# A Fourier layer split as 49 by 64 in place of 56 by 56, with two buffers for a low part, a shared buffer and a merged addition

## The chip, the cores and the metric

The kernel runs on one core of one Trainium2 chip. The metric is the device time of one execution in microseconds. Before the change it is 1770.43 us, the median of three runs (1767.99 to 1770.92).

## What is computed

```python
X = np.fft.rfft(x, axis=1)                # x: (8, 3136, 256) float32
Yr = Xr @ w_r - Xi @ w_i + b_r
Yi = Xr @ w_i + Xi @ w_r + b_i
Yr = np.sign(Yr) * np.maximum(np.abs(Yr) - lam, 0.0)   # lam = 0.01; Yi alike
y = np.fft.irfft(Yr + 1j * Yi, n=3136, axis=1)
h = np.maximum(y @ w_in, 0.0)             # 256 -> 1024
gate = sigmoid(conv(h))                   # three taps along the sequence
out = (h * gate) @ w_out                  # 1024 -> 256
```

The real transform runs over 3136 points of each of 8 batches and 256 columns. The spectrum is mixed by a complex 256 by 256 matrix, thresholded and transformed back. A gated feed-forward block with a convolution of three taps follows.

## The kernel before, in words

**The transform by matrices.** 3136 = 56 x 56. A transform of 3136 points is done as two short ones: `stage1` (L239) transforms over one index of 56 points, with two columns j of the other index at once (112 rows), and writes 28 frequencies u to the DRAM array sc1. `stage2` (L273) transforms over the other index for one u at a time, by plain float32 matmuls whose stationary operand is the data and whose moving operand is the table t2 (128 columns). `mix` (L291) multiplies by the complex matrix in three products (c = 2, 0, 1), in float32r with a high and a low part of each operand (fh and fl, wmix_hi and wmix_lo), 36 matmuls of 256 columns; it adds the biases, thresholds and splits the result v into sh and sl. `stage3` (L324) is the first half of the way back, 12 matmuls, and writes to the DRAM array sc2. `stage4` (L416) reads sc2 across the u, does the second half and leaves the sequence of one batch in SBUF as yh and yl.

**Work items.** A group of stage 1 takes JC = 4 columns j, so a batch has 28/4 = 7 groups, each with two matmuls of 512 columns (L245) into one PSUM buffer, two copies on ACT (L246), and one store from a1 to sc1 (L247). An item (b, g) of stages 2, mix and 3 takes UG = 4 of the 28 u: 7 items per batch, 56 in all. Its input a2 is loaded from sc1 by L270; since an item needs all j of its batch, the first load of a batch waits for the last store of stage 1 of that batch. Stage 4 has 7 groups per batch, each with a load of z2 (L419) through three buffers, 8 matmuls (L423), a copy on ACT (L429) and a subtraction on DVE (L430).

**Thresholding (L305 to L321).** p1 holds the common product ps[2] plus the bias, one addition for the real and one for the imaginary part (L309); four additions over 64 rows form v (L313). ACT computes r = relu(v - lam) (L318), DVE ends with v = min(v + lam, r) (L319), ACT casts it to sh (L320) and POOL subtracts to sl (L321). p1, r and sl have one buffer each, v and sh two.

**Order.** The loop (L373) runs over the items with stage 2 of item `it`, mix of `it - 1` and stage 3 of `it - 3`; new stage-1 groups are asked for ahead of the items that need them (L386). A scheduler then fixes the order of each engine from these priorities; each engine works its list strictly in order. All loads and stores go through SP's list, where a DMA waits for its data or buffer and holds back those behind it. The weights are split in the background (`later`, L207). A head (`stage1_head`, L249) does batch 0's groups at once with all of its tiles in SBUF.

**The feed-forward part** runs in steps of `up` (L432, 12 matmuls of 450 columns) and `down` (L463, 21 matmuls of 256), 224 steps, with a stage-4 group of the next batch in three of eight steps until the batch is done. At its start stand the groups of batch 0 and two of batch 1.

Of the kernel before, what the change touches and what calls it, by code (L numbers as in the profile page):

```python
# [9 lines left out]
F32 = mybir.dt.float32  # L10
F32R = mybir.dt.float32r
# [7 lines left out]
B, S, D, FF = 8, 3136, 256, 1024  # L19
R = 56  # L20
U = 28
SL = 57
SP = 64
H = 28
LAM = 0.01
UG = 4
NG = U // UG
JC = 4
P = 128
# [5 lines left out]
def _tables():  # L35
    n = np.arange(R)
    u = np.arange(U)

    f = np.zeros((R, 2, U))
# [3 lines left out]
    f[:, 1, 0] = np.where(n % 2 == 0, 1.0, -1.0)  # L43
    fwd1 = np.zeros((2, R, U, 2, 2))
    for h in range(2):
        fwd1[h, :, :, :, h] = f.transpose(0, 2, 1)

    g = np.transpose(f, (1, 2, 0)).copy()
    g[:, 1:, :] *= 2.0
    g /= S  # L50
    inv2 = np.zeros((2, 2 * U, R, 2))
    for i in range(2):
        inv2[i, :, :, i] = g.reshape(2 * U, R)
    fwd2 = np.zeros((2, R, U, 2, SP))
    inv1 = np.zeros((2, SP, U, 2, R))
    for uu in range(U):
        for s in range(SL):
            if uu == 0:
                c = 0 if s < 29 else 1
                k = R * s if s < 29 else 28 + R * (s - 29)  # L60
                th = 2 * np.pi * ((k * n) % S) / S
                sn, cs = np.sin(th), np.cos(th)
                edge = k in (0, S // 2)
                if edge:
                    sn = np.zeros(R)
                    cs = np.round(cs)
                w = 1.0 if edge else 2.0
                fwd2[c, :, 0, 0, s] = cs
                fwd2[c, :, 0, 1, s] = -sn
                inv1[0, s, 0, c, :] = w * cs  # L70
                inv1[1, s, 0, c, :] = -w * sn
            elif s < R:
                k = uu + R * s
                th = 2 * np.pi * ((k * n) % S) / S
                sn, cs = np.sin(th), np.cos(th)
                sg = 1.0 if k <= S // 2 else -1.0
                fwd2[0, :, uu, 0, s] = cs
                fwd2[1, :, uu, 0, s] = sn
                fwd2[0, :, uu, 1, s] = -sn * sg
                fwd2[1, :, uu, 1, s] = cs * sg  # L80
                inv1[0, s, uu, 0, :] = cs
# [6 lines left out]
    return {
        "fwd1": fwd1.transpose(1, 0, 2, 3, 4).reshape(2 * R, 2 * R).astype(np.float32),
        "fwd2": fwd2.reshape(2 * R, U * 2 * SP).astype(np.float32),  # L90
        "inv1": inv1.reshape(2 * SP, U, 2, 2, H).transpose(0, 1, 4, 3, 2).reshape(2 * SP, U * 2 * R).astype(np.float32),
        "inv2": inv2.reshape(2 * R, 2 * R).astype(np.float32),
    }
# [3 lines left out]
def spectral_ffn_kernel(ctx: ExitStack, tc: tile.TileContext, x, w_r, w_i, b_r, b_i,  # L97
                        w_in, conv_w, w_out, fwd1, fwd2, inv1, inv2, out):
    nc = tc.nc
    K1, K2 = 2 * R, 2 * SP  # L100
# [3 lines left out]
    sc2 = [dram.tile([K1, U, D], F32, name=f"sc2_{b}") for b in range(B)]  # L104

    cst = ctx.enter_context(tc.tile_pool(name="cst", bufs=1))


    i2 = cst.tile([K1, K1], F32, name="i2")
    cw = cst.tile([P, 3, NF], F32, name="cw")  # L110
# [6 lines left out]
    with ExitStack() as ab:  # L117
# [12 lines left out]
        f1 = c1.tile([K1, P], F32, name="f1")[:, 0:K1]  # L130
        t2 = c1.tile([K1, U, K2], F32, name="t2")
# [136 lines left out]
        def load_a2(b, g):  # L268
            a2 = a2p.tile([K1, UG, D], F32, name="a2")
            ld = nc.sync.dma_start(a2, sc1[b].rearrange("(u q) j d -> (q j) u d", q=4)[:, g * UG:(g + 1) * UG, :])  # L270
            return a2, ld

        def stage2(g, a2):  # L273

            fh, fl = [wkf.tile([P, NT, 3, UG, SP], F32R, name=nm) for nm in ("fh", "fl")]
            d = wkf.tile([P, NT, UG, SP], F32, name="d", bufs=DB)
            for t in range(NT):
                ps = ps2.tile([P, UG, 2, SP], F32, name="ps_s2")
                for k in range(UG):
                    nc.tensor.matmul(ps[:, k], a2[:, k, t * P:(t + 1) * P], t2[:, g * UG + k, :],  # L280
                                     start=(k == 0), stop=(k == UG - 1), skip_group_check=True)
# [6 lines left out]
            nc.vector.tensor_tensor(fl[:, :, 2], d, fh[:, :, 2].bitcast(F32), op=ALU.subtract)  # L288
            return fh, fl

        def mix(xs):  # L291
# [15 lines left out]
            half = (slice(0, SP), slice(SP, K2))  # L307
            for c in range(2):
                nc.vector.tensor_tensor(p1[:, c], ps[2], bias[:, c], op=ALU.add)  # L309
            for c in range(2):  # L310
# [13 lines left out]
        def stage3(b, g, s):  # L324

            sh, sl, _ = s
            ps = psa.tile([K1, UG, D], F32, name="ps_s3")
            for k in range(UG):
                u = g * UG + k
                for n, (lt, rh) in enumerate(((i1_hi, sh), (i1_hi, sl), (i1_lo, sh))):  # L330
                    nc.tensor.matmul(ps[:, k, :], lt[:, u, :], rh[:, k, :], start=(n == 0), stop=(n == 2))  # L331
# [73 lines left out]
    JG = 4  # L405
# [135 lines left out]
```

## Time and profile before

| what | value |
|---|---|
| median of three runs | 1770.43 us (1767.99 to 1770.92) |
| the profiled execution | 1769.05 us, span 1767.3 us |
| mean granted clock of TensorE | 0.995 |
| busy share: PE, weight load, DVE, ACT, POOL | 98%, 92%, 86%, 70%, 8% |
| stage 1, head and after | 14 and 98 matmuls, the last one near 475 us |
| spectral part | to about 549 us |
| first `up` | 574 us |
| DMA, whole span | 164.63 MB, mean 93 GB/s |

PE is TensorE's matmul queue, PEld its weight loads, DVE VectorE, ACT ScalarE, POOL GpSimd, SP the engine whose queue issues the DMAs. In a group of instructions `a<-b` means that tile a is written from tile b; L280 is line 280. "Idle before" names what released an engine after it had stood still. A plain float32 matmul shows as two records. The chain that ended last follows, from the end backwards, at each step what the work had waited for.

### The profile page before, as it was taken

How to read it: one execution, taken by the hardware profiler on the slowest of the kernel's cores; microseconds unless marked ns; L12 is line 12 of the kernel's file. 1: busy time of each engine (PE TensorE's matmuls, PEld its weight loads, DVE VectorE, ACT ScalarE, POOL GpSimd, SP SyncE). 2: the span in 40 equal slices, each digit the busy share in tenths (PEclk: the TensorE clock that was granted, in tenths of full speed). 3: DMA queues.
4: the chain of work that ended last, by engine and by line, in shares of the span. 5: the costliest groups of instructions: out<-in, count | busy, mean ns of one | idle time of the engine just before them, and what ended most of it. 6: DMA issues, size and time to landing. Idle time of an engine off the chain costs nothing.

```text
span 1767.3 us, 29387 instructions
## 1 busy us (share of the span) xinstructions
PE 1731.0 (98%) x12096; PEld 1621.6 (92%) x12096; DVE 1524.3 (86%) x1820; ACT 1229.1 (70%) x1590; POOL 134.7 (8%) x60
## 2 busy tenths in 40 slices
PE   6899999999998999999999999999999999999999
PEld 2788888888998999999999999999999999999998
DVE  2899999998896988988888888888888888888887
ACT  2667777776665777777777777777777777777766
POOL 0122222222232000000000000000000000000000
PEclk8999999999999999999999999999999999999999
DMA  9777677677534110111111011111101111100001
GB/s 263 216 230 236 196 232 216 192 230 228 164 111 136 43 43 22 32 53 53 32 53 53 22 55 51 49 46 52 43 22 43 53 43 43 42 22 22 22 22 42
DMA packets 107382, 164.63 MB, mean 93 GB/s; under 512 B 8816, under 2 KB 86000, under 8 KB 107248
## 3 DMA queue, kind: packets, MB, share of 16 engines
q1 hardware_dynamic: 107248, 162.74, 30.9%
q8 instruction: 96, 1.57, 0.4%
q14 instruction: 38, 0.31, 0.1%
HBM read 85.65 MB, written 77.07 MB: 92 GB/s over the span
## 4 chain that ended last, share of the span: by engine, by line
PE 93%; DMA 3%; DVE 1%; ACT 1%; issue 0%; SPq 0%; ACTq 0%
PE acc L470 31%; PE ps_h L442 31%; PE ps_mx L304 12%; PE ps_s L423 5%; PE ps_s L280 5%; PE ps_s L331 4%; PE ps_s L245 4%; DMA i_raw<-in_inv_dram 2%; DMA z<-sc 1%; DMA sc<-ha 0%; DMA a<-sc 0%; DMA sc<-a 0%; ACT a L246 0%; DVE cw L212 0%; DVE yl L430 0%
## 5 line engine op out<-in xcount | busy, mean ns | idle before, releaser
L470 PE MATMUL acc<-wout,gh 128*128 128x256 f32 x3136 | 567.0, 280 | 0.0
L451 DVE SCALAR_TENSOR_TENSOR c<-h,cw,c 128x896 f32<-128x896 f32 x448 | 513.1, 1147 | 47.3 <-ACT c L449 46.3
L442 PE MATMUL ps_h<-yh,win 128*128 128x450 f32 x1792 | 551.0, 368 | 0.1
L470 PEld LDWEIGHTS acc<-wout,gh 128*128 128x128 f32 x3136 | 493.7, 188 | 6.5
L470 PE MATMUL acc<-wout,gl 128*128 128x256 f32 x1568 | 437.6, 281 | 0.0
L444 ACT ACTIVATE h<-ps_h 128x900 f32<-128x900 f32 x224 | 207.7, 927 | 254.8 <-PE ps_h L442 254.8
L442 PEld LDWEIGHTS ps_h<-yh,win 128*128 128x128 f32 x1792 | 338.7, 189 | 26.4 <-DVE yl L430 0.8
L442 PE MATMUL ps_h<-yl,win 128*128 128x450 f32 x896 | 329.2, 367 | 0.0
L470 PEld LDWEIGHTS acc<-wout,gl 128*128 128x128 f32 x1568 | 293.7, 188 | 0.1
L457 DVE TENSOR_TENSOR gl<-c,gh 128x896 fp32r<-128x896 f32 x224 | 243.1, 1089 | 53.6 <-ACT gh L456 50.1
L453 DVE TENSOR_TENSOR c<-h,c 128x896 f32<-128x896 f32 x224 | 243.6, 1088 | 46.9 <-ACT c L452 46.7
L456 ACT CAST gh<-c 128x896 fp32r<-128x896 f32 x224 | 209.8, 942 | 49.4 <-DVE c L453 49.4
L452 ACT ACTIVATE c<-c 128x896 f32<-128x896 f32 x224 | 213.3, 952 | 23.9 <-DVE c L451 21.0
L304 PE MATMUL ps_mx<-wmix_lo,fh 128*128 128x256 f32 x672 | 202.2, 301 | 0.0
L304 PE MATMUL ps_mx<-wmix_hi,fh 128*128 128x256 f32 x672 | 196.9, 294 | 0.5 <-DVE v L313 0.3
L304 PE MATMUL ps_mx<-wmix_hi,fl 128*128 128x256 f32 x672 | 188.7, 282 | 1.3 <-DVE fl L288 1.2
L442 PEld LDWEIGHTS ps_h<-yl,win 128*128 128x128 f32 x896 | 168.9, 189 | 11.0
L449 ACT ACTIVATE c<-h,cw 128x896 f32<-128x896 f32 x168 | 175.5, 1044 | 2.6 <-DVE gl L457 0.2
L321 POOL TENSOR_TENSOR sl<-v,sh 128x1024 fp32r<-128x1024 f32 x56 | 134.5, 2402 | 423.1 <-PE ps_s L331 300.0
L313 DVE TENSOR_TENSOR v<-ps_mx,p 64x512 f32<-64x512 f32 x224 | 154.0, 688 | 3.3
L304 PEld LDWEIGHTS ps_mx<-wmix_lo,fh 128*128 128x128 f32 x672 | 126.4, 188 | 12.3 <-issue 12.3
L304 PEld LDWEIGHTS ps_mx<-wmix_hi,fl 128*128 128x128 f32 x672 | 126.0, 188 | 11.8 <-issue 9.9
(84 smaller groups left out, 2023.0 us busy)
## 6 DMA issues: line engine op xcount, KB each, us to landing
a<-sc SPq DMA_DIRECT2D x56, 448.0 KB, 5.0
sc<-z SPq DMA_DIRECT2D x56, 448.0 KB, 3.3
z<-sc SPq DMA_DIRECT2D x56, 448.0 KB, 3.8
xr<-in_x_dram SPq DMA_DIRECT2D x55, 448.0 KB, 4.7
out_dram<-o SPq DMA_DIRECT2D x27, 896.0 KB, 4.0
sc<-a SPq DMA_DIRECT2D x49, 448.0 KB, 4.9
sc<-ha SPq DMA_DIRECT2D x7, 448.0 KB, 7.5
win_bits<-in_moe_w_in_dram SPq DMA_DIRECT2D x4, 512.0 KB, 7.6
```

The source lines that it names most:

```text
L304: nc.tensor.matmul(ps[c][:, k, :], lt, rh, start=(n == 0), stop=(n == len(mm) - 1))
L313: nc.vector.tensor_tensor(v[dst, :, k, :], ps[c][src], p1[src, c], op=ALU.add)
L321: SL_ENG.tensor_tensor(sl, v, sh.bitcast(F32), op=ALU.subtract)
L442: nc.tensor.matmul(ps[:, a, 0:CH + 2], lt, rh, start=(n == 0), stop=(n == len(mm) - 1))
L444: nc.scalar.activation(h, ps[:, :, 0:CH + 2], AF.Relu)
L449: nc.scalar.mul(c, h[:, :, 0:CH], cw[:, 0, f:f + 1])
L451: nc.vector.scalar_tensor_tensor(c, h[:, :, k:k + CH], cw[:, k, f:f + 1], c, op0=ALU.mult, op1=ALU.add)
L452: nc.scalar.activation(c, c, AF.Sigmoid)
L453: nc.vector.tensor_tensor(c, h[:, :, 1:CH + 1], c, op=ALU.mult)
L456: nc.scalar.copy(gh, c)
L457: nc.vector.tensor_tensor(gl, c, gh.bitcast(F32), op=ALU.subtract)
L470: nc.tensor.matmul(acc[m // 2][:, m % 2, :], lt[:, sl], rh[:, f, :], start=(f == 0 and n == 0 and m % 2 == 0), stop=(f == NF - 1 and n == ...
```

## The change

The sequence is split as 49 x 64. Stage 1 now transforms over 49 points (R) with 98 rows and 32 pairs of columns j (H), which makes 8 groups of 4 per batch, 64 in all. There are 25 frequencies u, 0 to 24. Since 49 is odd, none but u = 0 is special: u = 1 to 24 fill 6 whole items per batch, and u = 0 of four batches is gathered into one item, which makes 8 x 6 + 2 = 50 items. The second index has 64 points, so that stage 2 has 128 rows and stage 3 writes 128 rows (64 rows are read for u = 0). Stage 4 reads 100 rows (25 x 4), has a moving operand of 98 columns and 8 groups per batch. 

Besides, one addition over 1024 elements, with ps[2] read twice, takes the place of the two of L309; sl gets a second buffer; r takes the memory of p1. The rule that asks for new stage-1 groups lets two per item in at first and four per three items later, for one and a half and then one.

```diff
-R = 56
-U = 28
-SL = 57
+R = 49
+R2 = 64
+U = 24
 SP = 64
-H = 28
+H = 32
...
         def load_a2(b, g):
-            a2 = a2p.tile([K1, UG, D], F32, name="a2")
-            ld = nc.sync.dma_start(a2, sc1[b].rearrange("(u q) j d -> (q j) u d", q=4)[:, g * UG:(g + 1) * UG, :])
+            a2 = a2p.tile([KQ, UG, D], F32, name="a2")
+            if g < NG:
+                rows = slice(g * 4 * UG, (g + 1) * 4 * UG)
+                ld = nc.sync.dma_start(a2, sc1[b][rows].rearrange("(u q) j d -> (q j) u d", q=4))
+            else:
+                for k in range(UG):
+                    ld = nc.sync.dma_start(a2[0:R2, k, :], sc1[b + k][4 * U:K1].rearrange("q j d -> (q j) d"))
             return a2, ld
...
                 for k in range(UG):
-                    nc.tensor.matmul(ps[:, k], a2[:, k, t * P:(t + 1) * P], t2[:, g * UG + k, :],
+                    rows, u = (KQ, g * UG + k) if g < NG else (R2, U)
+                    nc.tensor.matmul(ps[:, k], a2[0:rows, k, t * P:(t + 1) * P], t2[0:rows, u, :],
                                      start=(k == 0), stop=(k == UG - 1), skip_group_check=True)
...
-            for c in range(2):
-                nc.vector.tensor_tensor(p1[:, c], ps[2], bias[:, c], op=ALU.add)
+            nc.vector.tensor_tensor(p1, ps[2].unsqueeze(1).broadcast_to([K2, 2, UG // 2, D]), bias, op=ALU.add)
...
-            sl = wk.tile([K2, UG, D], F32R, name="sl", bufs=1)
-            r = wk.tile([K2, UG, D], F32, name="r", bufs=1)
+            sl = wk.tile([K2, UG, D], F32R, name="sl")
+            r = p1.rearrange("p c k d -> p (c k) d")
...
-            nc.sync.dma_start(sc2[b][:, g * UG:(g + 1) * UG, :], z1)
+            if g < NG:
+                nc.sync.dma_start(sc2[b][:, g * UG:(g + 1) * UG, :], z1)
+            else:
+                for k in range(UG):
+                    nc.sync.dma_start(sc2[b + k][:, U, :], z1[:, k, :])
...
-        AHEAD = NG + 3
         items = [(b, g) for b in range(B) for g in range(NG)]
+        for b in (0, UG):
+            items.insert(items.index((b + UG - 1, 0)), (b, NG))
...
-            while p1 < n_it and p1 < min(it + AHEAD, NG + 2 + it + it // 2):
-                stage1(*items[p1])
+            while p1 < min(len(firsts), NQ + 2 + 2 * it, NQ + 5 + 4 * it // 3):
+                stage1(*firsts[p1])
                 p1 += 1
```

**What the change moves.** On PE, at the turn from batch 4 to batch 5: before, stage 3 of an item (L331), one matmul of stage 1 of the next batch (L245), then the first stage 2 of batch 5 (L280, reading the tile a_3803) and its mix (L304).

```order
L331 MATMUL ps_s_3990<-sh,i_hi 112x256
L331 MATMUL ps_s_3990<-sl,i_hi 112x256
L331 MATMUL ps_s_3990<-sh,i_lo 112x256
L245 MATMUL ps_s_4009<-xr,f_113 112x512
L280 MATMUL ps_s_4026<-t_114,a_3803 128x128 x4
L280 MATMUL ps_s_4035<-t_114,a_3803 128x128 x4
L304 MATMUL ps_mx_4048<-wmix_hi,fh 128x256
```

The same place in the new order; L342 is stage 3, L251 stage 1, L292 stage 2 (a_3438 is the first tile of batch 5).

```order
L342 MATMUL ps_s_3847<-sh,i_hi 128x256
L342 MATMUL ps_s_3847<-sl,i_hi 128x256
L342 MATMUL ps_s_3847<-sh,i_lo 128x256
L251 MATMUL ps_s_3326<-xr,f_113 98x512
L251 MATMUL ps_s_3429<-xr,f_113 98x512
L342 MATMUL ps_s_3952<-sh,i_hi 128x256
L292 MATMUL ps_s_3669<-t_114,a_3438 128x128 x4
L292 MATMUL ps_s_3678<-t_114,a_3438 128x128 x4
L251 MATMUL ps_s_3432<-xr,f_113 98x512
L342 MATMUL ps_s_3952<-sl,i_hi 128x256
```

Stage 2 of the new batch has moved up to the end of the old batch's stage 3, with no mix left in front of it. On SP at the same place, the x load, the last two stores of stage 1 of batch 5 (to sc_5), the store of z (to sc_4) and the loads of the first items of batch 5:

```order
L247 DMA sc_5_62<-a_3685 112x1024
L334 DMA sc_4_69<-z_3788 112x1024
L236 DMA xr<-in_x_dram 112x1024
L247 DMA sc_5_62<-a_3793 112x1024
L270 DMA a_3803<-sc_5_62 112x4x256
L270 DMA a_3911<-sc_5_62 112x4x256
L334 DMA sc_4_69<-z_3895 112x1024
```

And in the new order, with L253 the store of stage 1, L346 that of z and L278 the load:

```order
L242 DMA xr<-in_x_dram 98x1024
L253 DMA sc_5_62<-a_3312 98x1024
L346 DMA sc_4_69<-z_3754 128x1024
L278 DMA a_3438<-sc_5_62 128x4x256
L278 DMA a_3544<-sc_5_62 128x4x256
L242 DMA xr<-in_x_dram 98x1024
L278 DMA a_3664<-sc_5_62 128x4x256
```

The load still stands close behind the last store; what moved is how much PE has queued between the two. On DVE, late in the spectral part, before (L309 the two bias additions, L319 the end of the item before them, L288 a subtraction of stage 2):

```order
L309 TENSOR_TENSOR p_5733<-ps_mx_5696,bias 128x512 x2
L319 SCALAR_TENSOR_TENSOR v<-v,r 128x1024
L288 TENSOR_TENSOR fl<-d,fh 128x2x256
L313 TENSOR_TENSOR v<-ps_mx_5694,p_5733 64x2x256 x2
L313 TENSOR_TENSOR v<-ps_mx_5695,p_5733 64x2x256 x2
```

The same in the new order (L330 ends an item, L320 is the merged addition of the next):

```order
L330 SCALAR_TENSOR_TENSOR v<-v,p_5071 128x1024
L300 TENSOR_TENSOR fl<-d,fh 128x2x256
L320 TENSOR_TENSOR p_5164<-ps_mx_5127,bias 128x1024
L324 TENSOR_TENSOR v<-ps_mx_5125,p_5164 64x2x256 x2
L324 TENSOR_TENSOR v<-ps_mx_5126,p_5164 64x2x256 x2
```

The end of an item now stands ahead of the next item's bias addition, and the two additions are one. Counted over the whole order of PE, the matmuls that stand between the start of the last stage-1 matmul of a batch and the first stage 2 that reads that batch's own item (without that first matmul itself) are:

| batch | before: mix, stage 3, stage 1, stage 2 | new: mix, stage 3, stage 1, stage 2 |
|---|---|---|
| 1 | 56, 12, 2, 0 | 0, 24, 4, 0 |
| 2 | 62, 24, 3, 8 | 36, 13, 2, 0 |
| 3 | 62, 24, 3, 8 | 19, 22, 3, 2 |
| 4 | 62, 24, 3, 8 | 41, 24, 2, 0 |
| 5 | 62, 24, 3, 8 | 0, 18, 3, 0 |
| 6 | 62, 24, 3, 8 | 34, 24, 2, 0 |
| 7 | 62, 24, 0, 8 | 34, 24, 0, 2 |

Six items stand behind the last stage 1 in the new order. At the turn to the feed-forward part ten stage-4 groups (8 of batch 0, two of batch 1) stand in front of the first `up`, for nine before.

More of the change, by code (lines that the diff above doesn't have):

```diff
@@ L42, in _tables @@
     f[:, 1, :] = -np.sin(ang)
-    f[:, 1, 0] = np.where(n % 2 == 0, 1.0, -1.0)
-    fwd1 = np.zeros((2, R, U, 2, 2))
+    fwd1 = np.zeros((R, 2, 2 * R))
     for h in range(2):
-        fwd1[h, :, :, :, h] = f.transpose(0, 2, 1)
+        for uu in range(1, U + 1):
+            for c in range(2):
+                fwd1[:, h, (uu - 1) * 4 + c * 2 + h] = f[:, c, uu]
+        fwd1[:, h, 4 * U + h] = f[:, 0, 0]
     g = np.transpose(f, (1, 2, 0)).copy()
@@ L50, in _tables @@
     g /= S
-    inv2 = np.zeros((2, 2 * U, R, 2))
+    g = np.roll(g, -1, axis=1)
+    inv2 = np.zeros((2, 2 * (U + 1), R, 2))
     for i in range(2):
[L53 to L57, printed above, removed]
+        inv2[i, :, :, i] = g.reshape(2 * (U + 1), R)
+    fwd2 = np.zeros((2, R2, U + 1, 2, SP))
+    inv1 = np.zeros((2, SP, U + 2, 2, R2))
+    for uu in range(U + 1):
+        at = (uu - 1) % (U + 1)
+        for s in range(SP):
+            k = uu + R * s
+            th = 2 * np.pi * ((k * n2) % S) / S
+            sn, cs = np.sin(th), np.cos(th)
@@ new lines, in _tables @@
+                fwd2[0, :, at, 1, s] = -sn
+                inv1[0, s, at, 0, :] = w * cs
+                inv1[1, s, at, 0, :] = -w * sn
+            else:
+                sg = 1.0 if k <= S // 2 else -1.0
+                fwd2[0, :, at, 0, s] = cs
+                fwd2[1, :, at, 0, s] = sn
+                fwd2[0, :, at, 1, s] = -sn * sg
+                fwd2[1, :, at, 1, s] = cs * sg
+                inv1[0, s, at, 0, :] = cs
+                inv1[0, s, at, 1, :] = sn
+                inv1[1, s, at, 0, :] = -sg * sn
+                inv1[1, s, at, 1, :] = sg * cs
@@ L86, in _tables @@
+    inv1[:, :, U + 1] = inv1[:, :, U]
     inv1[:, :, 1::2] = inv1[::-1, :, 1::2]
     return {
[L89 to L92, printed above, removed]
+        "fwd1": fwd1.reshape(2 * R, 2 * R).astype(np.float32),
+        "fwd2": fwd2.reshape(2 * R2, (U + 1) * 2 * SP).astype(np.float32),
+        "inv1": inv1.reshape(2 * SP, U + 2, 2, 2, H).transpose(0, 1, 4, 3, 2).reshape(2 * SP, (U + 2) * 2 * R2).astype(np.float32),
+        "inv2": inv2.reshape(4 * (U + 1), 2 * R).astype(np.float32),
@@ L99, in spectral_ffn_kernel @@
     nc = tc.nc
-    K1, K2 = 2 * R, 2 * SP
+    K1, K2, KQ, KI = 2 * R, 2 * SP, 2 * R2, 4 * (U + 1)
     dram = ctx.enter_context(tc.tile_pool(name="dram", bufs=1, space=DRAM))
     sc1 = [dram.tile([K1, H, D], F32, name=f"sc1_{b}") for b in range(B)]
-    sc2 = [dram.tile([K1, U, D], F32, name=f"sc2_{b}") for b in range(B)]
+    sc2 = [dram.tile([KQ, U + 1, D], F32, name=f"sc2_{b}") for b in range(B)]
     cst = ctx.enter_context(tc.tile_pool(name="cst", bufs=1))
-    i2 = cst.tile([K1, K1], F32, name="i2")
+    i2 = cst.tile([KI, 112], F32, name="i2")[:, 0:K1]
     cw = cst.tile([P, 3, NF], F32, name="cw")
@@ L130, in spectral_ffn_kernel @@
         f1 = c1.tile([K1, P], F32, name="f1")[:, 0:K1]
-        t2 = c1.tile([K1, U, K2], F32, name="t2")
+        t2 = c1.tile([KQ, U + 1, K2], F32, name="t2")
         cmx.tile([P, 96], F32, name="pad")
@@ L165, in load_inv1 @@
         def load_inv1(g):
-            raw = stg.tile([K2, UG, K1], F32, name="i1_raw", tag="raw", bufs=2)
-            sl = slice(g * UG, (g + 1) * UG)
+            sl = slice(g * UG, min((g + 1) * UG, U + 2))
+            raw = stg.tile([K2, sl.stop - sl.start, KQ], F32, name="i1_raw", tag="raw", bufs=2)
             nc.sync.dma_start(raw, inv1v[:, sl, :])
@@ L338, in spectral_ffn_kernel @@
         nc.scalar.activation(warm, warm, AF.Sigmoid)
-        AHEAD = NG + 3
         items = [(b, g) for b in range(B) for g in range(NG)]
+        for b in (0, UG):
+            items.insert(items.index((b + UG - 1, 0)), (b, NG))
         n_it = len(items)
+        firsts = [(b, jc) for b in range(B) for jc in range(NQ)]
         WP0, CW_IT = 3, 9
         a2s = {}
-        p1 = NG
+        p1 = NQ
         load_f1()
@@ L348, in spectral_ffn_kernel @@
             xh = []
-            for p in range(NG):
+            for p in range(NQ):
                 xr, ld = load_x(hx, 0, p, parts=2 if p == 0 else 1, tag=f"hx{p}")
@@ L368, in spectral_ffn_kernel @@
         wk.tile([P, 72], F32, name="pad", bufs=1)
-        i1_hi = cab.tile([K2, U, K1], F32R, name="i1_hi")
-        i1_lo = cab.tile([K2, U, K1], F32R, name="i1_lo")
+        i1_hi = cab.tile([K2, U + 2, KQ], F32R, name="i1_hi")
+        i1_lo = cab.tile([K2, U + 2, KQ], F32R, name="i1_lo")
         background = later()
@@ L385, in spectral_ffn_kernel @@
                 stage3(*items[it - 3], ss.pop(it - 3))
-            while p1 < n_it and p1 < min(it + AHEAD, NG + 2 + it + it // 2):
-                stage1(*items[p1])
+            while p1 < min(len(firsts), NQ + 2 + 2 * it, NQ + 5 + 4 * it // 3):
+                stage1(*firsts[p1])
                 p1 += 1
@@ L416, in stage4 @@
     def stage4(b, jg, y):
-        z2 = zio.tile([K1, JG, D], F32, name="z2")
+        z2 = zio.tile([KI, JG, D], F32, name="z2")
         nc.sync.dma_start(z2, sc2[b].rearrange("(j q) u e -> (q u) j e", q=4)[:, jg * JG:(jg + 1) * JG, :])
```

49 lines of the change are left out of this document (18 added, 31 removed).

## The prediction

> **What bounds the kernel now.** I read the page first, then the busy time of each engine over three stretches, then the chain of work that ended last inside one period of the spectral part, and last the waits of the DMA queue.
>
> ```profile
> span 1767.3 us, 29387 instructions
> ```
>
> ```profile
> 150.00:450.00 300.00, 300.00 (x2234) 267.29 (x2233) 279.59 (x450) 215.45 (x344) 78.85 (x33) 1.00 0.73 216
> 505.00:535.00 30.00, 30.00 (x261) 30.00 (x260) 29.66 (x48) 21.30 (x34) 9.90 (x5) 1.00 0.32 97
> 574.00:1767.00 1193.00, 1188.88 (x8147) 1143.87 (x8146) 1034.19 (x1026) 855.76 (x998) 0.00 (x0) 1.00 0.13 40
> ```
>
> The columns are length, then busy time of PE, weight load, DVE, ACT and POOL, the clock, and the DMA share. PE is the bound from 150 us to the end: it never stands still in the first two stretches and stands 4 us in the third. DVE is close behind: 279.59 of 300 while stage 1 still runs, 29.66 of 30 once it is over, 1034 of 1193 in the feed-forward part. So the change is worth the PE time that it takes away or adds, less any wait that it puts in front of PE.
>
> The chain shows what one work item costs PE.
>
> ```profile
> 437.89 0.86 PE ps_s L245 x2
> 438.75 3.04 PE ps_mx L304 x26
> 441.80 1.42 PE ps_s L331 x12
> 443.21 0.86 PE ps_s L245 x2
> 444.07 1.78 PE ps_s L280 x16
> 445.86 1.17 PE ps_mx L304 x10
> ```
>
> ```profile
> 505.31 2.80 PE ps_mx L304 x24
> 512.72 2.80 PE ps_mx L304 x24
> ```
>
> An item is 36 mix matmuls (3.04 + 1.17 = 4.21), 12 of stage 3 (1.42) and 8 of stage 2 (1.78; the trace counts each plain float32 matmul twice): 7.41 us, which is also the period from 505.31 to 512.72, where no stage 1 is left. One stage-1 group is two matmuls of 0.86; with it the period is 9.13.
>
> **Fewer items, more groups.** Items go from 56 to 50: 6 x 7.41 = 44.5 us less. The matrices keep 128 rows or columns where they had 128 or 112, and an item of u = 0 runs the same count of matmuls, so the price of one stays. Stage-1 groups go from 56 to 64; 14 more matmuls stand behind the head (112 against 98): 14 x 0.86 = 12.0 us more. Stage 4 has 64 groups for 56.
>
> ```profile
> 755.72 1.77 PE ps_s L423 x16
> ```
>
> A group has 8 matmuls with 98 moving columns in place of 112. If time followed the columns, a group would take 1.55 us and the term would be zero. But stage 2 moves 128 columns and takes 1.78 for the same count, so 112 and 128 cost alike and something other than the columns sets the time. I take 1.77: 8 x 1.77 = 14.2 us more, zero being the other end. Net so far: -44.5 + 12.0 + 14.2 = **-18.3 us**.
>
> **The first stage 2 of each batch.** It needs the last stage 1 of its batch: matmul, copy on ACT, store to DRAM, load from DRAM. This chain's rows:
>
> ```profile
> 301.06 1.02 PE L245 MATMUL ps_s<-xr,f 112*112 112x512 f32 x2
> ...
> 302.12 0.59 ACT L246 COPY a<-ps_s 112x512 f32<-112x512 f32 x1 [0.56 <-PE ps_s L245]
> ...
> 302.73 0.30 SPq L247 DMA_DIRECT2D sc<-a  x1
> ```
>
> ```profile
> 99.89 3.08 DMA sc<-a
> 102.97 0.02 issue
> 102.98 4.20 DMA a<-sc
> ```
>
> ```profile
> 412.01 0.30 SPq L247 DMA_DIRECT2D sc<-a  x1
> 416.40 0.85 SPq L270 DMA_DIRECT2D a<-sc  x2
> ```
>
> ```profile
> a<-sc SPq DMA_DIRECT2D x56, 448.0 KB, 5.0
> ```
>
> ```profile
> SPq L270 <- DMA sc<-a: 25.4, 7, 4.3
> PE ps_s L280 <- DMA a<-sc: 1.1, 1, 1.1
> ```
>
> From the matmul's start to the store's issue: 1.67 us. The store: 3.08 at best (batch 1), 4.39 at 412 us; over the seven batches SP waited 25.4 / 7 = 3.6 and issued for some 0.5, so 4.1 on average. The load: 4.20 at best, 5.0 in the median. The chain is 8.95 at best, 11.1 with the slower pair, 10.7 with the means. Today PE has 15 us of other work queued between the two ends in most batches (62 mixes, 24 of stage 3, 3 of stage 1, 8 of stage 2, and the first matmul itself: 7.25 + 2.84 + 2.58 + 1.78 + 0.86), and only batch 1 waits, 1.1 us. In the new order the counts of the table above give, at 0.117, 0.118, 0.86 and 0.22 us each and with the first matmul's own 0.86: batch 1 7.1, batch 2 8.3, batch 3 8.7, batch 4 10.2, batch 5 5.6, batch 6 9.4, batch 7 8.1. Since PE works in order, it stands for what is missing. At 10.7: 3.6 + 2.4 + 2.0 + 0.5 + 5.1 + 1.3 + 2.6 = 17.5; at 8.95: 6.9; at 11.1: 20.3. I take 17.5 less the 1.1 that is there today: **+16.4 us**. While SP waits for the store, the next x load and the store of z1 are queued behind it; the x tile is used groups later, so I count nothing for that, up to the same chain once more if a group were starved.
>
> **The clock after a gap.**
>
> ```profile
> 548.73 0.37 PE L331 MATMUL ps_s<-sh,i_hi 128*112 128x256 f32 x1 [2.12 <-ACT sh L320]
> ```
>
> ```profile
> 545.00:550.00 5.00, 2.88 (x22) 2.66 (x21) 3.87 (x5) 2.98 (x3) 1.20 (x1) 0.92 0.28 88
> 550.00:555.00 5.00, 5.00 (x35) 5.00 (x35) 2.01 (x1) 2.15 (x3) 1.17 (x1) 0.74 0.02 7
> ```
>
> After a wait of 2.12 us in a stretch where PE was busy 2.88 of 5, the granted clock was 0.74 over the next 5 us: 5 x 0.26 = 1.3 us lost. The waits of batches 1 and 5 are clearly longer, the other three of over 2 us about as long but out of full work. I take two: **+2.6**, between 0 and 5 x 1.3 = 6.5. The Trainium skill's page "TensorE: Matmul & The Clock Gate" (section "What's actually happening") has the clock fall only after a whole idle window of about 3.4 us; that fits two falls here, but this trace shows one after 2.12 us, which speaks for five.
>
> **Head, turn to the feed-forward part, merged addition.**
>
> ```profile
> 20.00:32.00 12.00, 1.98 (x4) 0.54 (x4) 4.07 (x7) 2.12 (x5) 0.00 (x0) 0.79 0.97 333
> ```
>
> ```profile
> 563.90 2.02 PE ps_s L423 x16
> 565.93 0.02 issue
> 565.94 6.21 DMA z<-sc
> 572.16 0.14 issue
> 572.29 2.01 PE ps_s L423 x16
> ```
>
> ```profile
> 507.29 1.28 DVE L309 TENSOR_TENSOR p<-ps_mx,bias 128x512 f32<-128x512 f32 x2
> 508.48 1.22 DVE L319 SCALAR_TENSOR_TENSOR v<-v,r 128x1024 f32<-128x1024 f32 x1
> 509.61 0.69 DVE L288 TENSOR_TENSOR fl<-d,fh 128x512 fp32r<-128x512 f32 x1
> 510.21 2.81 DVE L313 TENSOR_TENSOR v<-ps_mx,p 64x512 f32<-64x512 f32 x4
> ```
>
> The head stores 8 tiles in place of 7 with the DMA engines full (0.97): the same bytes cost 0, by count 12/7 = 1.7; I take 0.9. At the turn, ten stage-4 groups in place of nine come through three z2 buffers: a round of load and group is 6.21 + 2.01, a third of it 2.74, of which 1.77 is counted: +1.0, and at most one whole load, 6.2. Two additions of 512 take 1.19 us from start to start, one pass over 1024 takes 1.13: 0.06 saved, which counts only where DVE is full, in the six items behind the last stage 1: -0.4. Were the repeated read as slow per element as the additions over 64 rows (2.81/4 = 0.70 for 512), it would be 1.40, or +1.3 in all. The second buffer of sl and the shared p1/r cost nothing: POOL's sl is off the chain, and the operation that ends an item on DVE now stands ahead of the next item's addition, with two d and two fl as cover for ACT's relu; without that cover DVE would stand, by an estimate from its own pass over 1024, some 1.1 us in each of the six items. Larger tables add only load bytes in the first 100 us.
>
> **The sum:** -18.3 + 16.4 + 2.6 + 0.9 + 1.0 - 0.4 = +2.2 us on the profiled execution's 1769.05, or 1771.3; that execution was 1.4 under the median of the three runs, so the forecast is **1772 us**, no change. I count 0.2% (3.5 us) as what a measurement of this kernel can tell from no change.
>
> **Rivals.** *The chain is short.* If stores and loads take what they took for batch 1 (3.08 and 4.20), the waits are 6.9 and one gap lowers the clock: -18.3 + 5.8 + 1.3 + 0.9 + 1.0 - 0.4 = -9.7, 1759 us. For it: the one chain quoted from end to end, that of batch 1, was this short. Against it: SP's mean wait of 3.6. Zero cost for stage 4 would take 14 more.
>
> *The chain is long and the clock falls each time (slower).* Place: PE in front of the first stage 2 of batches 1, 2, 3, 5, 7. Price: 20.3 - 1.1 for the waits, 6.5 for five falls: -18.3 + 19.2 + 6.5 + 0.9 + 1.0 - 0.4 = +8.9, 1778 us. It decides from a chain of about 10.9 us on, since each microsecond more costs nearly seven. For it: the pair at 412 us, and more DMA bytes per item: a2 and z1 grow to 512 KB, x and a1 stay at 448 KB x 7/8 x 4/3 groups. Against it: the DMA share of 0.73 leaves room.
>
> *Transfers of 98 and 100 rows are slow (slower still).* Every transfer here has 112, 128 or 64 rows. If the new row counts cost the chain 1.3 us more (12.0), the waits are 26.6 - 1.1; with 6.5 for the clock, 1.7 at the head and 2.7 at the turn it is +17.7, 1787 us. The Trainium skill's page "DMA: Bandwidth & Descriptors" (section "Why a DMA increments its semaphore by 16 and not by 1") says that a transfer uses the largest number of engines up to 16 that divides its outermost size: 14 for 98 rows, 10 for 100. By that rule a 98-row tile puts 392/14 = 28 KB on each engine, as 448/16 does now, so only z2 would be slower, and this rival would lose most of its price. No run here shows which engines carry a transfer.
>
> **Chances.** The forecast 0.34, short chain 0.32, long chain 0.23, slow rows 0.11. Hence faster 0.32, same 0.34, slower 0.34. The range of 1758 to 1784 leaves out the upper case's upper half and the lower end of the short chain.
>
> **What would show it.** Right: PE waits for a<-sc in front of stage 2 in six or seven places, 15 to 20 us in all; 9.13 us periods with one stage-1 group as now; stage 4 at 1.77 us per group; the feed-forward part longer by 12 us. Wrong: few such waits (the gain stays), stage-4 groups near 1.55, or PE standing for DVE or xr elsewhere in the spectral part.

## The result and the profile after

The changed kernel takes 1809.9 us (median of four runs, 1808.88 to 1811.33) against 1770.68 us of the kernel before beside it: a ratio of 1.0223, 95% interval 1.0205 to 1.0241. It is slower by 39 us, where 1772 with a range of 1758 to 1784 was forecast. The profiled execution took 1811.33 us, its span is 1809.5.

First the same stretches as before, for the changed kernel (length, busy time of PE, weight load, DVE, ACT and POOL, clock, DMA share):

```profile
150.00:450.00 300.00, 284.31 (x1960) 237.55 (x1959) 267.23 (x371) 196.69 (x315) 70.74 (x29) 0.99 0.63 208
505.00:535.00 30.00, 28.11 (x229) 27.00 (x229) 26.49 (x37) 19.48 (x34) 7.16 (x3) 1.00 0.53 175
603.00:1809.00 1206.00, 1202.15 (x8256) 1157.42 (x8254) 1033.60 (x1033) 855.28 (x1005) 0.00 (x0) 1.00 0.13 40
```

Between 150 and 450 us PE now stands for 15.7 us where it stood for none. The first `up` starts at 602.50 in place of 574.07, and what follows lasts 13.8 us longer (1207.0 against 1193.2). So 28.4 us were added in the part whose work the sum had made 31 us shorter (six items fewer, 14 matmuls of stage 1 and one group of stage 4 more): some 59 us have to be found there.

The waits of PE between 100 and 500 us (what waited, for what: total, times, longest):

```profile
PE ps_s L251 <- ACT a L252: 16.2, 15, 4.6
PE ps_mx L316 <- DVE v L324: 2.8, 3, 1.3
PE ps_s L292 <- DMA a<-sc: 2.4, 4, 1.0
```

The load in front of the first stage 2, which the forecast made the dear wait, is 2.4 us here. Most of the waiting is stage 1's own: its next matmul waits for the ACT copy out of its only PSUM buffer. The copy can itself be held up from farther back: in the longest wait, 4.57 us at 461.86, it waited for a store out of stage 1's two a1 buffers, which took 10.48 us to land (450.67 to 461.15). Where PE loses time is seen in the windows around three starts of a batch and around the turn to the feed-forward part:

```profile
95.00:120.00 25.00, 19.90 (x83) 12.03 (x83) 12.87 (x21) 12.71 (x20) 4.70 (x2) 0.80 0.75 249
355.00:385.00 30.00, 25.14 (x150) 19.06 (x149) 21.31 (x28) 17.43 (x26) 7.09 (x3) 0.94 0.61 208
450.00:470.00 20.00, 15.43 (x94) 12.97 (x93) 14.35 (x23) 9.12 (x17) 2.37 (x1) 0.83 0.80 236
560.00:610.00 50.00, 44.12 (x231) 42.69 (x230) 18.29 (x23) 17.73 (x19) 4.69 (x2) 0.66 0.36 114
```

The first three lose 14.5 us of idle time and, with busy time multiplied by the missing part of the clock, 4.0 + 1.5 + 2.6 = 8.1 us to the low clock; the turn loses 5.9 and 15.0. In the kernel before, the same first three windows lose 2.4 us of idle time and none to the clock.

One of these starts in detail, batch 5. PE, then POOL, ACT and DVE between 365 and 372 us (start, length, operation; in brackets the idle time before and what ended it):

```profile
365.51 1.02 PE L251 MATMUL ps_s<-xr,f 98*98 98x512 f32 x2
370.63 1.10 PE L251 MATMUL ps_s<-xr,f 98*98 98x512 f32 x2 [3.50 <-ACT a L252]
```

```profile
366.81 2.34 POOL L332 TENSOR_TENSOR sl<-v,sh 128x1024 fp32r<-128x1024 f32 x1 [6.99 <-ACT sh L331]
```

```profile
369.47 0.63 ACT L193 ACTIVATE wout_e<-wout_e 128x512 int32<-128x512 int32 x1 [2.74 <-DVE wout_e L192]
370.01 0.57 ACT L252 COPY a<-ps_s 98x512 f32<-98x512 f32 x1
```

```profile
365.51 0.42 DVE L191 TENSOR_SCALAR wout_e<-wout_bits 128x512 int32<-128x512 int32 x1
365.97 1.23 DVE L320 TENSOR_TENSOR p<-ps_mx,bias 128x1024 f32<-128x1024 f32 x1
367.11 2.33 DVE L192 TENSOR_SCALAR wout_e<-wout_e 128x512 int32<-128x512 int32 x1
```

Read from the bottom: a small step of the weights' splitting, L192, takes 2.33 us (its neighbour of the same shape, L191, 0.42) while POOL's subtraction of sl runs beside it, and ends 0.3 us behind that. ACT's next operation needs it, the copy of stage 1 stands behind that in ACT's list, and PE's next stage-1 matmul, in PE's strictly ordered list, stands 3.50 us. The order at a batch's start and POOL's subtraction meet here, and the experiments take them apart.

### The profile page after: what moved, and what is told of

Its sections match the earlier page's. It is cut to its first block, busy times and chain, and to the rows that moved or that the text cites. A ratio compares the mean times of both kernels' runs of the same rounds, so it can differ in the third digit from the quotient of the medians.

```text
span 1809.5 us, 28682 instructions
## 1 busy us (share of the span) xinstructions
PE 1749.5 (97%) x11872; PEld 1615.1 (89%) x11872; DVE 1507.1 (83%) x1707; ACT 1207.5 (67%) x1565; POOL 121.1 (7%) x54
## 4 chain that ended last, share of the span: by engine, by line
PE 79%; DVE 8%; issue 5%; DMA 5%; ACT 2%; POOL 1%; SPq 0%; ACTq 0%; DVEq 0%; POOLq 0%
PE ps_h L459 31%; PE acc L487 31%; PE ps_s L440 7%; PE ps_mx L316 5%; DVE v L324 3%; PE ps_s L251 3%; PE ps_s L292 3%; PE ps_s L342 2%; DMA i_raw<-in_inv_dram 1%; DVE p L320 1%; DMA sc<-a 1%; POOL sl L332 1%; DVE v L330 1%; DVE fl L298 1%; DMA a<-sc 1%
## 5 line engine op out<-in xcount | busy, mean ns | idle before, releaser
L459 PEld LDWEIGHTS ps_h<-yh,win 128*128 128x128 f32 x1792 | 339.9, 190 | 26.2 <-DVE yl L447 0.4
L316 PE MATMUL ps_mx<-wmix_hi,fh 128*128 128x256 f32 x600 | 180.6, 303 | 5.0 <-DVE v L324 3.5
L316 PE MATMUL ps_mx<-wmix_hi,fl 128*128 128x256 f32 x600 | 174.9, 296 | 0.3 <-DVE fl L300 0.3
L316 PE MATMUL ps_mx<-wmix_lo,fh 128*128 128x256 f32 x600 | 173.6, 291 | 0.0
L332 POOL TENSOR_TENSOR sl<-v,sh 128x1024 fp32r<-128x1024 f32 x50 | 120.9, 2417 | 450.8 <-ACT sh L331 450.8
L251 PE MATMUL ps_s<-xr,f 98*98 98x512 f32 x224 | 122.3, 628 | 27.8 <-ACT a L252 19.1
L324 DVE TENSOR_TENSOR v<-ps_mx,p 64x512 f32<-64x512 f32 x200 | 137.5, 688 | 5.8 <-PE ps_mx L316 0.2
L440 PEld LDWEIGHTS ps_s<-i,z 100*128 100x128 f32 x1024 | 134.6, 207 | 5.0 <-DVE yl L447 3.5
```

The costliest lines, as they stand in the source:

```text
L251: nc.tensor.matmul(ps, f1, xr[:, j:j + 2, :], start=True, stop=True)
L316: nc.tensor.matmul(ps[c][:, k, :], lt, rh, start=(n == 0), stop=(n == len(mm) - 1))
L324: nc.vector.tensor_tensor(v[dst, :, k, :], ps[c][src], p1[src, c], op=ALU.add)
L440: nc.tensor.matmul(ps[:, t, j * K1:(j + 1) * K1], z2[:, j, t * P:(t + 1) * P], i2, start=(j == 0), stop=(j == JG - 1), skip_group_check=True)
L459: nc.tensor.matmul(ps[:, a, 0:CH + 2], lt, rh, start=(n == 0), stop=(n == len(mm) - 1))
```

## The experiments

All times are medians; the ratio is to the kernel before, run beside each on the same chip.

**The three small edits undone on the new split.**

```diff
-            nc.vector.tensor_tensor(p1, ps[2].unsqueeze(1).broadcast_to([K2, 2, UG // 2, D]), bias, op=ALU.add)
+            for c in range(2):
+                nc.vector.tensor_tensor(p1[:, c], ps[2], bias[:, c], op=ALU.add)
...
-            sl = wk.tile([K2, UG, D], F32R, name="sl")
-            r = p1.rearrange("p c k d -> p (c k) d")
+            sl = wk.tile([K2, UG, D], F32R, name="sl", bufs=1)
+            r = wk.tile([K2, UG, D], F32, name="r", bufs=1)
```

> The new split with the thresholding of before: two bias additions, r and sl with one buffer each of their own. Theory 'shared buffer' (p1 held until the end of the item makes DVE, ACT and DVE wait for each other, and PE behind them): most of the 40 us goes, 1780 us or less. Theory 'batch boundary' (the missing cover in front of the first stage 2 of each batch, with the clock falling behind the gaps): the covers are no longer here, so it stays at 1805 to 1815 us. Theory 'turn' (the low clock while stage 4 runs in a row in front of the first up, about 12 us): stays too, unless the turn's waits come out otherwise.

Measured: 1796.06 us, 1.0142 (1.0124 to 1.0160). The three edits cost 14 us; 25 us remain with the new split alone. PE stands as long between 100 and 500 us as in the changed kernel (24.0 us for 25.2), but other waits lead, the load first (L343 is stage 3 there, L345 its copy):

```profile
PE ps_s L292 <- DMA a<-sc: 9.5, 5, 3.3
PE ps_s L343 <- ACT z L345: 6.8, 5, 3.4
PE ps_s L251 <- ACT a L252: 2.0, 4, 0.8
```

With one buffer of sl, too, L192 stands beside POOL's subtraction at the start of batch 5 (2.38 us, from 358.99); there it is the copy of z and with it stage 3 that come late, and PE stands 3.43 us.

**The three edits on the old split.** The reverse lines in the kernel before.

> The split of before (56 x 56) with the merged addition, the shared p1 and r and the two buffers of sl. 'Shared buffer': slower than before by 20 us or more, 1790 us. 'Batch boundary' and 'turn': the covers are those of before (15.3 us), so within 5 us of 1770.

Measured: 1788.85 us, 1.0100 (1.0081 to 1.0118). They cost 18 us there too, where PE's order still has the work of before between a batch's last stage 1 and its first stage 2.

**Stage 4 with 112 moving columns.**

```diff
-                nc.tensor.matmul(ps[:, t, j * K1:(j + 1) * K1], z2[:, j, t * P:(t + 1) * P], i2, start=(j == 0), stop=(j == JG - 1),
+                nc.tensor.matmul(ps[:, t, j * 112:(j + 1) * 112], z2[:, j, t * P:(t + 1) * P], i2w, start=(j == 0), stop=(j == JG - 1),
```

> The changed kernel with 112 moving columns in stage 4 (14 of them zeros, not read). If the low clock at the turn lasts because groups with 98 columns do not fill the array enough, the 24 us at half clock shrink to 3 or 7 and it gains 8 to 10 us, 1800 us, and groups still take 1.77. If the columns have nothing to do with it: 1810 us, or 14 us more if columns cost time (64 groups by 0.22).

Measured: 1807.81 us, 1.0198 (1.0171 to 1.0225), the four runs at 1799.65, 1806.94, 1808.68 and 1808.89. The profiled one is the first, and its clock was low only for short at the turn; the other three are near those of the changed kernel. So 14 more columns cost nothing, and whether they help the clock isn't settled: one run in four.

**Items that read the batch before.**

```diff
-                ld = nc.sync.dma_start(a2, sc1[b][rows].rearrange("(u q) j d -> (q j) u d", q=4))
+                ld = nc.sync.dma_start(a2, sc1[max(b - 1, 0)][rows].rearrange("(u q) j d -> (q j) u d", q=4))
```

> The changed kernel, but the items read stage 1's result of the batch before their own (batch 0 its own), so that no item waits for a store just made; the result is that of other data. 'Batch boundary': 20 to 30 us faster than the changed kernel, 1780 to 1790 us, with no wait of PE for the load and no fall of the clock between 100 and 500 us. 'Shared buffer': the many short waits stay, at most 5 us faster.

Measured: 1804.37 us, 1.0188 (1.0171 to 1.0204), a miss: the edit leaves the two gathered items of u = 0 reading their own batches. Its windows show the wait at just these two places:

```profile
200.00:250.00 50.00, 43.59 (x199) 28.08 (x198) 23.81 (x34) 25.74 (x40) 7.59 (x4) 0.80 0.65 207
480.00:520.00 40.00, 34.81 (x216) 29.51 (x214) 23.27 (x34) 19.67 (x32) 4.98 (x4) 0.83 0.35 124
```

The spacing of items named in the next expectation is that between the last mix matmuls of one item and the next, read from the same trace. The next two kernels move the gathered items too; they again compute with other data.

```diff
-                    ld = nc.sync.dma_start(a2[0:R2, k, :], sc1[b + k][4 * U:K1].rearrange("q j d -> (q j) d"))
+                    ld = nc.sync.dma_start(a2[0:R2, k, :], sc1[max(b + k - 1, 0)][4 * U:K1].rearrange("q j d -> (q j) d"))
```

> new_split_old_buf, with every load of items, those of u = 0 too, reading stage 1's result of the batch before its own (of batch 0 its own); it computes with other data. In prev_batch the gathered items of u = 0 still read their own batches and took the whole wait over (38.3 and 24.7 us from one item to the next). 'Batch start': the work runs dry at the start of every batch (the thresholding of the last item, the last groups of stage 1 one by one, store, load, refilling), 41 us in the seven places of new_split_old_buf, and all of it goes: 1755 to 1763 us, faster than before. As the prediction priced it (a wait for the chain alone, 16 us and some clock): 1775 to 1780 us.

> The same on the changed kernel itself, with p1 shared and the addition merged. 'Batch start' and 'shared buffer' add up: 36 us less than 1810, 1772 to 1778 us, that is some 15 us above old_buf_prev_all. If the shared buffer costs only where a batch starts: the same time as old_buf_prev_all.

Measured: 1763.38 us, 0.9971 (0.9958 to 0.9984), and 1770.29 us, 1.0005 (0.9995 to 1.0015): 33 and 40 us less than with the dependence. One row each, 100 to 500 us, of the changed kernel, of new_split_old_buf, of old_buf_prev_all and of prev_all:

```profile
100.00:500.00 400.00, 374.76 (x2542) 311.44 (x2541) 343.39 (x480) 253.76 (x410) 88.94 (x37) 0.97 0.62 206
```

```profile
100.00:500.00 400.00, 376.05 (x2585) 318.45 (x2585) 340.07 (x519) 258.81 (x416) 88.83 (x37) 0.98 0.63 207
```

```profile
100.00:500.00 400.00, 390.22 (x2811) 338.00 (x2810) 373.92 (x573) 272.75 (x440) 98.42 (x41) 1.00 0.66 212
```

```profile
100.00:500.00 400.00, 392.39 (x2825) 339.71 (x2823) 371.04 (x527) 270.53 (x440) 100.03 (x42) 1.00 0.67 215
```

Idle time of PE goes from 24.0 to 9.8 us with the three edits undone and from 25.2 to 7.6 with them, and the clock is whole. With the clock that is 21 and 26 us between 100 and 500 us, for 19 in the forecast (16.4 and 2.6); the rest of the 33 and 40 us stands at the turn and in PE's own work. These two kernels show what dependence and order cost together, not the wait alone: without the dependence the scheduler also spreads stage 1 out, with at most three of its matmuls between two mixes from the second item on, where the changed kernel has up to eight. "Between two mixes" here and below is from the end of one item's mix to the end of the next.

**r in its own buffer, one buffer of sl, the addition merged** (the last two lines of the first diff alone).

> The changed kernel with r in a buffer of its own and one buffer for sl, the merged addition kept. If it is the shared buffer that costs: 1793 to 1799 us, as with the three undone (1796). If it is the merged addition: 1807 to 1812 us.

Measured: 1803.09 us, 1.0193 (1.0170 to 1.0216), between the two. From new_split_old_buf it differs by the merged addition alone, and the intervals of the two ratios don't meet: on the new split the merged addition by itself costs some 9 us.

**On the old split one edit at a time:** r in p1; then the merged addition; then two buffers of sl.

> The kernel before with r put into p1, nothing else. If the shared buffer costs by itself: 1785 to 1792 us, as with the three edits together on the old split (1789). If the merged addition or the buffers of sl did it: 1768 to 1774 us.

> The kernel before with the merged addition alone. The three edits together cost 18 us on the old split and r in p1 alone 4. If the rest is the merged addition: 1780 to 1786 us, with longer waits of PE for p or v. If the edits cost only together (sl or the order that comes out): 1768 to 1774 us.

> The kernel before with two buffers of sl alone. If the rest is the merged addition: within 3 us of 1770. If the second buffer lets an order come out that costs: 1775 us or more.

Measured: 1772.89 us, 1.0029 (1.0018 to 1.0040); 1771.36 us, 1.0014 (1.0004 to 1.0023); 1791.79 us, 1.0127 (1.0114 to 1.0140). It is the second buffer of sl: +22 us alone, no less than the three together. The groups of DVE between 150 and 450 us, in the kernel before and then with two buffers of sl (busy time, mean ns of one):

```profile
L313 DVE TENSOR_TENSOR v<-ps_mx,p 64x512 f32<-64x512 f32 x132 | 90.8, 688 | 1.9
L288 DVE TENSOR_TENSOR fl<-d,fh 128x512 fp32r<-128x512 f32 x33 | 23.3, 705 | 0.1
```

```profile
L313 DVE TENSOR_TENSOR v<-ps_mx,p 64x512 f32<-64x512 f32 x124 | 85.1, 687 | 1.8
L288 DVE TENSOR_TENSOR fl<-d,fh 128x512 fp32r<-128x512 f32 x32 | 36.5, 1142 | 0.1
```

And POOL in both, at about 352 us:

```profile
351.90 2.37 POOL L321 TENSOR_TENSOR sl<-v,sh 128x1024 fp32r<-128x1024 f32 x1 [6.76 <-PE ps_s L331]
```

```profile
353.55 2.38 POOL L321 TENSOR_TENSOR sl<-v,sh 128x1024 fp32r<-128x1024 f32 x1 [7.28 <-ACT sh L320]
```

With one buffer POOL waits for PE's stage 3 to let sl go, and so runs beside the four additions that read PSUM, which it doesn't slow (0.69 us). With two it starts as soon as sh is there and runs beside the subtraction fl<-d,fh, whose inputs both lie in SBUF, and beside steps of the weights' splitting; these take up to 2.8 us in place of 0.4 to 0.7. The Trainium skill's page "SBUF — State Buffer" (section "SBUF: two separate sides") says that POOL and a DVE operation with two SBUF inputs, or in a two-port mode, exclude each other for a whole operation. The rows agree: 705 ns against 1142 for two SBUF inputs, no change where one input is PSUM. Of the splitting steps between 100 and 500 us, 14 take over 1 us with two buffers of sl, each of them beside POOL's subtraction; in the kernel before none does. PE's idle time in that stretch grows from 1.1 to 11.0 us, 6.0 of them in 13 waits for fl; the rest of the 22 us wasn't traced.

**The changed kernel with one buffer of sl,** nothing else undone.

> The changed kernel with one buffer of sl, the merged addition and p1's double use kept. If the second buffer, by which POOL's subtraction starts earlier and falls beside DVE operations that read SBUF alone, is the dear part of the three edits here as on the old split (22 of 18 us there): 1797 to 1803 us, with the subtraction fl<-d,fh back near 0.7 us. If the merged addition or p1 is it: 1806 to 1811 us.

Measured: 1799.92 us, 1.0186 (1.0161 to 1.0210). Against the changed kernel that is 10 us less by the medians and 6.5 by the ratios, whose intervals meet. So the second buffer of sl costs here too, though less than on the old split, and sl_one and r_own, which differ by p1's double use alone, can't be told apart. The subtraction over the whole run, in the changed kernel and here:

```profile
L300 DVE TENSOR_TENSOR fl<-d,fh 128x512 fp32r<-128x512 f32 x50 | 42.8, 856 | 2.4 <-ACT fh L299 1.4
```

```profile
L300 DVE TENSOR_TENSOR fl<-d,fh 128x512 fp32r<-128x512 f32 x50 | 36.8, 737 | 9.5 <-ACT fh L299 8.9
```

**More room for stage 1.** Between the end of one item's mix and the end of the next, the order of the changed kernel has mostly two matmuls of stage 1, one group, and where a batch starts 8, 4, 5, 7 and 5. Eight groups in 6.25 items are 2.6 matmuls per item. The next kernels give stage 1 a share of three PSUM banks:

```diff
-        ps1 = ab.enter_context(tc.tile_pool(name="ps1", bufs=1, space=PSUM))
-        ps2 = ab.enter_context(tc.tile_pool(name="ps2", bufs=2, space=PSUM))
+        ps2 = ab.enter_context(tc.tile_pool(name="ps2", bufs=3, space=PSUM))
...
-                ps = ps1.tile([K1, 2, D], F32, name="ps_s1")
+                ps = ps2.tile([K1, 2, D], F32, name="ps_s1", tag="ps_12")
...
-                ps = ps2.tile([P, UG, 2, SP], F32, name="ps_s2")
+                ps = ps2.tile([P, UG, 2, SP], F32, name="ps_s2", tag="ps_12")
```

> The same three banks in the changed kernel, with its buffers and merged addition. If the pile is the cause: 1763 to 1772 us, at prev_all's 1770 or a little below. Otherwise 1800 us or more.

> new_split_old_buf with stage 1 and stage 2 taking turns in three PSUM banks, where stage 1 had one and stage 2 two; nothing is left out. In the order of the changed kernel one buffer lets stage 1 in with two matmuls per item, too few for 8 groups in 6.25 items, and 5 to 8 matmuls pile up where a batch starts; with the shared banks the order has 4, 2, 2 and 21 to 34 us between the last stage 1 of a batch and its first stage 2. If that pile is the cause of the 41 us: 1755 to 1763 us, as with the data of the batch before (1763), faster than before. If the dependence through DRAM costs by itself whatever the order: 1785 us or more.

> Control: the kernel before with the three shared banks. It had 15 us of cover in most batches and lost some 2 us at each early item only, so no pile is there to be taken away: 1766 to 1772 us. If it gains as much as the new split does, the banks help whatever the split.

Measured: 1775.14 us, 1.0028 (1.0016 to 1.0040); 1770.15 us, 1.0003 (0.9995 to 1.0011); the control 1781.73 us, 1.0072 (1.0058 to 1.0086), slower than expected. The same work with the same dependence is 35 and 26 us faster with the three shared banks, while the banks alone make the old split 12 us slower. So the waits at the batch starts come from the order that one PSUM buffer for stage 1 leads to, and not from the split's work. Within that order two things changed at once: at most four matmuls of stage 1 stand between two mixes, and PE has more work between a batch's last stage 1 and its first stage 2. No run separates these two. The share kernel between 100 and 500 us:

```profile
100.00:500.00 400.00, 393.65 (x2827) 339.79 (x2826) 368.89 (x531) 271.34 (x438) 95.65 (x41) 1.00 0.66 212
```

> new_split_old_buf with stage 3 in two halves of one PSUM bank in place of one tile of two banks, and the bank that comes free as a second buffer of stage 1; stage 2 keeps its two. Nothing is left out. The order has 16 to 74 us between the last stage 1 of a batch and its first stage 2, and stage 4 among the last stage 3. If the pile at the batch start is the cause and the shared banks of old_buf_share cost 12 us by themselves (as on the old split): 1753 to 1763 us, faster than before. If each bank taken from another stage costs as much: about 1770 us.

Measured: 1786.31 us, 1.0097 (1.0083 to 1.0112), a miss: with still more cover it is slower than old_buf_share. DVE is full in it, and PE waits for DVE most:

```profile
100.00:500.00 400.00, 379.08 (x2680) 324.55 (x2679) 384.62 (x539) 261.54 (x459) 101.93 (x39) 0.99 0.63 208
```

```profile
PE ps_mx L316 <- DVE fl L300: 12.9, 13, 2.6
```

DVE's time goes into the weights' splitting: its steps take 88 us of this stretch, for 46 in old_buf_share. 23 of the 75 steps take over 1 us here, each beside POOL's subtraction of sl, and four of 76 there. No complete kernel tried beats the one before.

**Two groups of stage 4 moved behind the first up.**

> old_buf_share with the two stage-4 groups of batch 1 behind the first up, where they take the places of later ones: no work goes. If the run of stage-4 groups after the last stage 3 keeps the clock low, it is 3 to 6 us faster than old_buf_share; if the clock falls there anyway, within 2 us of it.

Measured: 1771.67 us, 1.0012 (1.0003 to 1.0022), within 2 us of old_buf_share. Over 520 to 570 us the clock is low in both, old_buf_share first:

```profile
520.00:570.00 50.00, 44.07 (x281) 42.71 (x282) 26.29 (x34) 23.64 (x24) 7.12 (x3) 0.83 0.39 125
```

```profile
520.00:570.00 50.00, 42.19 (x262) 39.81 (x261) 26.37 (x41) 20.89 (x23) 9.09 (x4) 0.80 0.35 109
```

## Why the prediction was wrong

In windows of 10 us up to the first `up`, three things can be summed for each profiled execution: PE's idle time, the busy time lost to a clock below full (busy time times the missing part), and what is left of the busy time, PE's work at full clock.

| kernel | 0 to 100: idle and clock | 100 to 500: idle, clock | 500 to `up`: idle, clock | work |
|---|---|---|---|---|
| before | 27.3 | 1.1, 0.0 | 7.1, 1.5 | 537.1 |
| changed | 24.9 | 25.2, 8.2 | 10.1, 13.1 | 521.0 |
| new_split_old_buf | 26.2 | 24.0, 6.4 | 6.3, 8.9 | 515.2 |
| old_buf_prev_all | 26.7 | 9.8, 0.0 | 5.4, 4.7 | 512.7 |
| old_buf_share | 24.1 | 6.5, 1.5 | 6.9, 7.2 | 514.6 |

Up to the first `up` the sum had 30.7 us less work, 17.9 us more waiting (16.4 + 0.9 + 1.0 - 0.4) and 2.6 us more of low clock. Measured are 16.1 us less work, 23.7 us more idle time and 20.8 us more of low clock.

**The clock, +2.6: the step that failed most.** It took the 1.3 us behind one gap of the kernel before, counted two such falls, and put nothing at the turn. The low clock costs 8.2 us between 100 and 500 us and 13.1 at the turn, where the kernel before lost 0.0 and 1.5. The chain of the changed kernel at the turn:

```profile
578.50 6.81 DMA z<-sc
...
585.45 17.36 PE ps_s L440 x80
602.80 7.05 PE ps_h L459 x24
```

The load is about as long as was allowed for (6.21). But five groups behind it take 17.36 us in place of 8.85 (5 x 1.77), and the first 24 matmuls of up 7.05 where they took 5.17 in the kernel before: 10 us, since the clock stays low.

```profile
574.30 5.17 PE ps_h L442 x24
```

**The net work, -18.3 us: too large a gain.** Ahead of the first up 16.1 us of work went in place of 30.7, and behind it 13.8 came in place of 12.4. The price of stage 4 was right: 1.77 us a group in spite of 98 columns.

```profile
609.85 1.76 PE ps_s L440 x16
```

The sum took every matmul at its pace in an unbroken row. Where PE has stood, one of stage 1 takes 1.10 us (at 370.63 above) in place of 0.86. In the kernels with few gaps, old_buf_prev_all and old_buf_share, 24.4 and 22.5 us of work are gone; the 6 to 8 us that are still missing there weren't traced.

**The first stage 2 of each batch, +16.4 us: the size was right, the wait only in part.** From the start of a batch's last stage-1 matmul to its first own stage 2, PE of the changed kernel is idle for 5.0, 2.0, 1.4, 0.9, 4.2, 2.1 and 1.7 us in batches 1 to 7. That is 17.3 us, where the forecast had 17.5, and 20.3 in new_split_old_buf. The chain was near the forecast's 10.7 us, too; its store and load for batch 6 of the changed kernel, and for batch 3, where the load is that of a gathered item:

```profile
430.11 5.60 DMA sc<-a
435.72 3.88 DMA a<-sc
```

```profile
236.05 3.03 DMA sc<-a
...
239.63 4.49 DMA a<-sc
```

But in the changed kernel only 2.4 us are waits for the load. The sum counted the next batch's stage-1 matmuls as work that covers the chain; these wait themselves, for the ACT copy out of their one PSUM buffer (16.2 us between 100 and 500 us). So the number was in part luck. The forecast also left out the idle time outside these stretches, some 8 us between 100 and 500 us. The table of matmuls in front of the prediction couldn't show it, nor the pile of stage 1 ahead of the last matmul: it counts only what stands behind that matmul.

**The second buffer of sl and the shared p1 at nothing: failed.** "POOL's sl is off the chain" was true of who waits for it, and wrong as a reason. The wait of POOL for PE in the kernel before had kept it beside operations that it doesn't slow. The three edits cost 14 us. Taken one after the other from new_split_old_buf, by the ratios, the merged addition costs 9 us, where -0.4 was set for it, p1's double use nothing that can be told from noise, and the second buffer of sl 6.5. On the old split each alone costs 2, 4 and 22: what such an edit costs depends on the order that comes out with it.

**Of the rivals** the slower one came nearest in its place, PE in front of the first stage 2, and in size for that part: 19.2 and 6.5 us, where idle time and clock grew by 24.1 and 8.2 between 100 and 500 us. It left out the turn, the work and sl. Slow rows of 98 and 100 don't show in the rows above: the load of z took 6.81 against 6.21, stores and loads of stage 1 3.03 to 5.60 and 3.88 to 4.49; the one store of 10.48 us stands alone, and its cause wasn't traced.

## What to carry to other kernels

When an order changes, ask of the work that is to cover a wait whether it can run itself: a stage-1 matmul that waits for its own buffer covers nothing. A producer that fitted at one group per item piles up at 1.3 if one buffer lets it in. Price a string of gaps by more than their idle time: here the low clock and the matmuls that start afresh cost as much again. And a second buffer for an engine off the critical path moves when that engine runs; ask what it will then run beside.

## What the hardware showed that was not expected

POOL's subtraction (2.4 us) holds up DVE operations that work on SBUF alone (L192 2.33 us in place of 0.42, even one of 128x8 elements, L196, 2.27 us at 99.12), and leaves those that read PSUM at 0.69.

The clock can stay low while PE is never idle. The turn of the changed kernel in steps of 5 us:

```profile
580.00:585.00 5.00, 2.28 (x19) 1.95 (x17) 2.67 (x7) 2.00 (x2) 0.00 (x0) 0.84 0.58 172
585.00:590.00 5.00, 4.55 (x21) 4.59 (x22) 0.00 (x0) 0.81 (x1) 0.00 (x0) 0.50 0.30 86
590.00:595.00 5.00, 5.00 (x26) 5.00 (x25) 2.06 (x2) 1.19 (x2) 0.00 (x0) 0.50 0.42 126
595.00:600.00 5.00, 5.00 (x25) 5.00 (x25) 1.02 (x1) 1.52 (x2) 0.00 (x0) 0.50 0.40 123
600.00:605.00 5.00, 5.00 (x21) 4.74 (x20) 2.07 (x2) 1.51 (x2) 0.00 (x0) 0.50 0.42 114
605.00:610.00 5.00, 5.00 (x22) 4.53 (x21) 1.62 (x2) 1.03 (x2) 0.00 (x0) 0.77 0.16 50
```

It comes back only some microseconds after `up` has begun at 602.50; through the groups of stage 4 it stays at 0.50 for over 15 us of busy PE. The page "TensorE: Matmul & The Clock Gate" of the Trainium skill ("What's actually happening") has it rise after about 3.4 us of sustained work; these rows differ. Why is open: in one of the four runs with 112 columns it was low for short stretches only; the times of the other three suggest that it was low for longer there.
